# Every engine and the DMA queue held to one planned order over four batches' attention and channel MLPs

## The chip, the cores and the metric

The kernel runs on one core of one Trainium2 chip. The metric is the device time of one execution in microseconds (us), the median of three runs. A difference under 0.2% (1.75 us here) can't be told from none in this kernel.

## The reference, cut to what matters

Four batches, 768 positions, 8 heads of 48 columns (384 columns in all). First a linear attention with a complex decay: a state of 48x48 per head is turned and shrunk at each position by a normalised complex number, takes up `k v^T`, and is read by `q`:

```python
mag = np.sqrt(a_re * a_re + a_im * a_im)
scale = np.minimum(mag, 0.999) / (mag + 1e-06)
for t in range(S):
    new_re = ar * S_re - ai * S_im
    new_im = ar * S_im + ai * S_re
    S_re, S_im = (new_re + kv, new_im)
    y[:, :, t] = np.einsum('bhd,bhde->bhe', q[:, :, t], S_re)
```

Then two mixers on `x` (the attention's output, batch x 768 x 384). The first adds a product of rank 32 over positions and runs a channel MLP of four times the width; the second mixes positions by cosines and sines of `x @ w_theta` and ends with a narrow channel product:

```python
u = x + (x^T @ U @ V)^T
x = u + np.maximum(u @ w_ch1, 0.0) @ w_ch2
theta = x @ w_theta
y = w_tok_r @ (x * cos(theta)) + w_tok_i @ (x * sin(theta))
u = x + y
out = u + np.maximum(u @ w_ch, 0.0)
```

## The kernel before, in words

**Attention.** Positions are cut into 24 chunks of 128 (six per batch) and handled in 12 pairs of chunks, three per batch. For each pair `load` brings `a_re`, `a_im`, `q`, `k` in by DMA, and `ew` turns the recurrence into ordinary products by some twenty elementwise steps that pass between VectorE (L337 products, L340 fused ones, L358 and L385 running products and sums) and ScalarE (L334: squares, reciprocal roots, arc tangent and sines, which need two different function tables). All pairs but one work in the same buffer `er`; pair 1 has its own in `wa` and `wb`. At a pair's end, four rotations (L337) and the gathers (L405, L407, L409, DMAs on SP) put `q` and `k` into the tile `QK`, one per chunk. Then `pe_steps` runs the chunk on TensorE: scores (L453), transposed keys (L469), the state's update (L492), the values read (L521), a transpose back (L535), and `gx` (L546), which gathers `x @ U`. After six chunks `g_steps` adds the product of rank 32 to the batch: one small VectorE step (L568), then six products (L576) and six sums (L581).

**Channel MLP.** `mlp_steps(b)` cuts a batch into three blocks of 256 positions. A block's prologue (L682) transposes `x`; then come six F units, each 18 matmuls into a hidden tile (L711), whose result ScalarE (`rh`, L716) and VectorE (`rl`, L721) split into a high and a low part, and six C units of 12 matmuls (L736) that bring it back to 384 columns. The 9 pieces of `w_ch1` and 12 of `w_ch2` come as 64-bit words and are unpacked by VectorE and ScalarE in pieces (`unpack`, L609 to L622, L311).

**What sets the order.** `startup` makes a list of steps, each with the engines that may run it, a size and what it reads and writes. `schedule` places them one after the other by a model of the engines (`COST`, `HOP`): among the steps that can start within a short window it takes the one of the lowest rank, and a rank is the step's depth in the list plus a number from the table `LEAD`. `fixed` then issues the steps in that order, and ties each engine in `HELD` to it. Before, the list holds batches 0 and 1 of the attention, the unpacking of the weights, and the MLP of batch 0 (`PLANNED = 2`), and `HELD` is VectorE, ScalarE and GpSimd. TensorE and the DMA queue of SP are ordered by the recording layer's own scheduler, by priorities (`lane`). So is everything in batches 2 and 3 (`attention(b)`) and in the MLPs of batches 1 to 3 (`mains(b)`).

**The second mixer** (L908 to L993) starts when the MLPs are nearly through. Its weights are unpacked (lane `w3`) after the last attention step, beside the MLPs of the last batches.

Of the kernel before, what the change touches and what calls it, by code (L numbers as in the profile page):

```python
# [56 lines left out]
PLANNED = 2  # L57
# [30 lines left out]
def schedule(steps, rank, bias, hop=HOP, window=400):  # L88
# [20 lines left out]
    while ready:  # L109
        cand, low = [], 1e18  # L110
        for n in ready:
# [33 lines left out]
        at[e], end[n] = en, en + hop[e]  # L145
# [14 lines left out]

def ranks(steps, names, lead, hop=HOP):
# [27 lines left out]
def attn_moe_kernel(tc, pk, qn, kn, v, are, aim, U, V, w1, w2, wth, wtr, wti, wch, out):  # L189
# [26 lines left out]
    stg = [xf[:, PLANNED * NC * C + i * 1536:PLANNED * NC * C + (i + 1) * 1536] for i in range(3)]  # L216
# [44 lines left out]
    wa = wp.tile([128, KF * C], F32, tag="w", name="wa")  # L261
    wb = wp.tile([128, KF * C], F32, tag="w", name="wb")
    e_store = dict(key="E", lo=er[:, 0:5], hi=er[:, 5:])

    w_store = dict(key="W", **{n: t[:, 0:5 * NR].rearrange("p (z n) -> p z n", z=5) for n, t in (("lo", wa), ("hi", wb))})
    for st in (e_store, w_store):
# [10 lines left out]
        G_.memset(st["rows"][8][:, :, 0:1], 0.0)  # L277

# [9 lines left out]
    def load(pr, st):  # L288
# [4 lines left out]
        for z, name in enumerate(("re", ROWS[zi], "q", "kk")):  # L293
# [4 lines left out]
            ops.append(step(f, "D", 1300, [], [(st["key"], st["names"].get(name, name))]))  # L298
        return ops

    def load_v(g):
# [6 lines left out]
        return step(f, "D", 1300, [], [f"vt{g % 2}"])  # L308
# [6 lines left out]
    def ew(pr, st):  # L315
# [44 lines left out]
        do("A", 6, K("A"), [("pc", pr)], lambda e: A_.copy(out=pcf[:, pr], in_=rows[4][:, :, T]))  # L360
# [27 lines left out]
        act(AF.Identity, n2, Bt, bias=b_magic, r=K("B"), w=K("n"), size=N + 100)  # L388
# [21 lines left out]
        for i, g in enumerate((2 * pr, 2 * pr + 1)):  # L410
            ew_state[g] = {}
            for cs, to, a, keys in ((1, "cd", n2, ("C", "D")), (0, "qk", Bt, ("q", "kk"))):
# [4 lines left out]
                do("D", 3250, kc + K(*keys), [f"qk{g % 2}{cs}"], lambda e, g=g, cs=cs: gather(e, g, cs))  # L417
# [10 lines left out]
    def pe_steps(g, gps):  # L428
# [47 lines left out]
        for i in range(2):  # L476
            m = bank()
# [723 lines left out]
```

## Time and profile before

| | us |
|---|---|
| median of 3 runs | 877.26 (877.17 to 877.90) |
| the profiled execution | 877.16, of which 875.4 are the span |
| TensorE busy in the span | 757.8 (87%) |
| VectorE busy | 524.9 (60%) |
| ScalarE busy | 453.3 (52%) |
| GpSimd busy | 124.3 (14%) |

Engines are PE (TensorE matmul), PEld (its weight loads, beside PE), DVE (VectorE), ACT (ScalarE), POOL (GpSimd) and SP (the DMA queue). In a row of stretches stand the stretch and its length, then the busy time of each engine with its instructions in brackets, then the granted clock of TensorE as a share of full speed, the mean busy share of the 16 DMA engines, and GB/s. A row of instructions gives start, length, engine, line, operation, tiles, shapes and count, and in square brackets the idle time before it and what ended it. A row of waits gives who waited for whom, the sum, the times and the longest. A matmul of 32-bit numbers is counted twice in the trace, one of the rounded 32-bit kind (L711, L736) once.

### The profile page before, as it was taken

Reading aid. Unit: us, or ns where it says so; the run is one execution under the profiler, and the core shown is the slowest. Engines: PE = TensorE matmul, PEld = TensorE weight load, DVE = VectorE, ACT = ScalarE, POOL = GpSimd, SP = SyncE. Lnnn points to the kernel's source line nnn. Section 1 sums busy time; section 2 is a strip of 40 time slices with the busy share of each in tenths; the row PEclk is TensorE's granted clock in tenths of the full one; section 3 lists DMA queues with packets and bytes.
Section 4 is the critical chain, followed back from the end, with each engine's and each line's share of the span. In section 5 each row is a group of like instructions: output and inputs, shape, how many; then the busy total and the mean of one; then the engine's idle time right before and its main releaser. Section 6 shows DMA issues by size and latency. Waiting matters only on the chain.

```text
span 875.4 us, 13800 instructions
## 1 busy us (share of the span) xinstructions
PE 757.8 (87%) x5338; PEld 717.1 (82%) x5338; DVE 524.9 (60%) x787; ACT 453.3 (52%) x772; POOL 124.3 (14%) x144
## 2 busy tenths in 40 slices
PE   0085588798989698989999999899999999999996
PEld 0075367686978698979999999899999999999996
DVE  6958988978819578668151587893244335253321
ACT  6965876757726976784433253444155345253300
POOL 1011010200000002010101000000064234133200
PEclk9995867999998799999999999999999999999999
DMA  9264463552332443540331137620060000000001
GB/s 259 75 177 122 115 184 82 161 165 75 91 91 55 118 119 82 128 113 19 95 87 27 55 128 266 212 99 1 1 218 1 28 28 27 1 28 28 28 28 31
DMA packets 105657, 79.78 MB, mean 91 GB/s; under 512 B 32912, under 2 KB 97424, under 8 KB 105584
## 3 DMA queue, kind: packets, MB, share of 16 engines
q1 hardware_dynamic: 105184, 78.62, 32.2%
q8 instruction: 44, 0.72, 0.3%
q10 hardware_dynamic: 400, 0.20, 0.1%
q14 instruction: 29, 0.24, 0.1%
HBM read 50.33 MB, written 9.44 MB: 68 GB/s over the span
## 4 chain that ended last, share of the span: by engine, by line
PE 59%; DVE 15%; ACT 10%; DMA 8%; issue 3%; SPq 3%; POOL 0%; DVEq 0%; ACTq 0%; POOLq 0%
PE h L711 10%; PE c L736 9%; PE h L971 9%; PE c L971 9%; PE m L920 4%; PE m L987 4%; DVE er L337 4%; PE m L453 4%; PE m L521 4%; DMA er<-in_pk_dram 2%; ACT er L334 2%; DVE er L340 2%; PE m L492 2%; DMA tok1l<-tl 2%; ACT L334 2%
## 5 line engine op out<-in xcount | busy, mean ns | idle before, releaser
L711 PE MATMUL h<-uh,w1h 128*128 128x256 f32 x432 | 126.8, 294 | 3.1 <-DVE rl L721 2.1
L711 PE MATMUL h<-ul,w1h 128*128 128x256 f32 x432 | 125.0, 289 | 1.4 <-DVE ul L692 1.4
L711 PE MATMUL h<-uh,w1l 128*128 128x256 f32 x432 | 124.3, 288 | 0.0
L463 POOL TENSOR_SCALAR_AFFINE_SELECT pt<-pt 128x512 f32<-128x512 f32 x48 | 45.8, 962 | 425.7 <-ACT pt L459 411.2
L337 DVE TENSOR_TENSOR er<-er 128x768 f32<-128x768 f32 (+1 forms) x99 | 101.9, 1054 | 4.0 <-ACT er L334 2.0
L736 PE MATMUL c<-w2h,rl 128*128 128x384 f32 x288 | 100.1, 348 | 4.1 <-DVE rl L721 4.0
L736 PE MATMUL c<-w2h,rh 128*128 128x384 f32 x288 | 95.6, 349 | 6.7 <-ACT rh L716 3.0
L736 PE MATMUL c<-w2l,rh 128*128 128x384 f32 x288 | 97.8, 342 | 1.2 <-DVE w2l L311 1.1
L721 DVE SCALAR_TENSOR_TENSOR rl<-h,rh 128x512 fp32r<-128x512 f32 x72 | 49.3, 685 | 78.8 <-ACT rh L716 78.8
L711 PEld LDWEIGHTS h<-uh,w1h 128*128 128x128 f32 x432 | 83.5, 193 | 6.1 <-DVE rl L721 2.7
L711 PEld LDWEIGHTS h<-ul,w1h 128*128 128x128 f32 x432 | 83.6, 193 | 1.9 <-DVE ul L692 1.6
L711 PEld LDWEIGHTS h<-uh,w1l 128*128 128x128 f32 x432 | 83.5, 193 | 0.4 <-issue 0.2
L334 ACT ACTIVATE er<-er 128x768 f32<-128x768 f32 x88 | 74.0, 845 | 16.0 <-DVE er L337 12.4
L716 ACT ACTIVATE rh<-h 128x512 fp32r<-128x512 f32 x72 | 42.8, 596 | 67.4 <-PE h L711 59.5
L453 PE MATMUL m<-QK 96*128 96x128 f32 x384 | 60.0, 303 | 10.9 <-DMA QK<-wa 8.8
L453 PEld LDWEIGHTS m<-QK 96*128 96x128 f32 x384 | 53.5, 211 | 15.3 <-issue 10.5
L340 DVE SCALAR_TENSOR_TENSOR er<-er 128x768 f32<-128x768 f32 x55 | 52.8, 966 | 20.2 <-ACT er L334 11.6
L469 PE MATMUL m<-ident,QK 96*128 96x96 f32 x160 | 22.8, 261 | 46.0 <-DMA QK<-er 44.3
L736 PEld LDWEIGHTS c<-w2h,rh 128*128 128x128 f32 x288 | 52.8, 190 | 9.5 <-ACT rh L716 3.9
L736 PEld LDWEIGHTS c<-w2h,rl 128*128 128x128 f32 x288 | 54.6, 190 | 6.5 <-DVE rl L721 6.0
L469 PEld LDWEIGHTS m<-ident,QK 96*128 96x128 f32 x160 | 18.2, 150 | 49.6 <-issue 48.6
L736 PEld LDWEIGHTS c<-w2l,rh 128*128 128x128 f32 x288 | 54.3, 189 | 2.3 <-DVE w2l L311 1.8
(209 smaller groups left out, 1741.3 us busy)
## 6 DMA issues: line engine op xcount, KB each, us to landing
er<-in_pk_dram SPq DMA_DIRECT2D x88, 192.0 KB, 3.7
QK<-er SPq DMA_DIRECT2D x88, 145.1 KB, 3.4
x<-in_moe_w_ch_dram SPq DMA_DIRECT2D x9, 512.0 KB, 4.4
vt<-in_v_dram SPq DMA_DIRECT2D x48, 96.0 KB, 2.7
x<-in_moe_w_ch_dram SPq DMA_DIRECT2D x12, 384.0 KB, 3.4
st<-in_moe_w_tok_i_dram SPq DMA_DIRECT2D x6, 768.0 KB, 5.6
st<-in_moe_w_tok_r_dram SPq DMA_DIRECT2D x6, 768.0 KB, 4.2
out_dram<-x SPq DMA_DIRECT2D x23, 192.0 KB, 2.3
```

Source lines behind the costliest of these rows:

```text
L334: do("A", size, r, w, lambda e: A_.activation(out=out, in_=in_, func=func, **kw), tab)
L337: do("V", size, r, w, lambda e: V_.tensor_tensor(out=out, in0=in0, in1=in1, op=op))
L340: do("V", size, r, w, lambda e: V_.scalar_tensor_tensor(out=out, in0=in0, scalar=scalar, in1=in1, op0=op0, op1=op1))
L453: PE.matmul(ps[:, hh * T:(hh + 1) * T], lhsT=st["QK"][:, h, 1, 0:T], rhs=st["QK"][:, h, 0, 0:T], start=True, stop=True)
L463: G_.affine_select(out=pt, in_=pt, pattern=[[0, 4], [1, T]], compare_op=ALU.is_ge, fill=0.0, base=0, channel_multiplier=-1)
L469: PE.transpose(ps[:, hh * 96:(hh + 1) * 96], st["QK"][:, 4 * i + hh, 1, 0:T], ident[0:96, 0:96])
L521: PE.matmul(st["y"][64 * z:64 * z + 64, r * T:(r + 1) * T], lhsT=wide(old_w if k else vt_w, h), rhs=st["QK"][:, h, 0, 0:T] if k else st[f" ...
L711: PE.matmul(ps[:, f, :], lhsT=a[:, k, fs], rhs=u[:, k, :], start=(k == 0 and i == 0), stop=(k == NJ - 1 and i == 2))
L716: A_.activation(out=rh, in_=rts[n, p], func=AF.Relu)
L721: V_.scalar_tensor_tensor(out=rl, in0=ps, scalar=0.0, in1=r32(rh), op0=ALU.max, op1=ALU.subtract)
L736: PE.matmul(chs[n, t][:, 0:C], lhsT=r[:, f, t * T:(t + 1) * T], rhs=w[:, k, :], start=(k == 0 and i == 0), stop=(k == KF - 1 and i == 2))
L971: PE.matmul(ps[k][:, 0:C], lhsT=z[:, 2 * part + o, k * 128:(k + 1) * 128], rhs=w[:, s, ts], start=(s == 0 and part == 0 and j == 0), stop= ...
```

## The change

`PLANNED` becomes 4: the list holds the attention of all four batches and all four MLPs, and `attention` and the calls of `mains` fall away. `HELD` now has TensorE and SP too, so all five queues follow one order until the MLP of batch 3 is through. The table `LEAD` is new, with a number pair for every job of the longer list.

Smaller parts: DMA steps have a time to landing of their own in the model, and some costs in it are other (GpSimd's select, the transposes, the unpacking's first step); a scores tile is taken only while another tile of its pool stays free; new keys (`gord`, `fo`, `co`, the block's number in `u`) keep steps of one kind in turn; the copies of `x` in batches 2 and 3 name the staging space of the weights that lies under them (`stages`); `wa` and `wb` are declared at the size that they use. One step of each pair, the rounding of the angle (L388, 768 columns), may now run on VectorE: in the new order 7 of 12 do.

```diff
-    'l0': (17.6, 55.3), 'e0': (1.2, 0.1), 'p0': (-49.1, -22.6), 'u': (-11.1, 38.3), 'x0': (283.2, 62.0),
...
+    'l0': (692.3, 517.6), 'e0': (-3475.0, 1033.3), 'p0': (-2365.3, -705.0), 'u': (1406.8, -988.4),
...
-PLANNED = 2
+STAGED = 2
+
+PLANNED = 4
...
-                if not free:
+
+                if len(free) < 1 + (new[0][0] == "ps" and len(new[0]) > 2):
                     continue
...
-        at[e], end[n] = en, en + hop[e]
+        at[e], end[n] = en, en + (steps[n][5] if e == "D" and steps[n][5] else hop[e])
...
+    def stages(b, c):
+
+        i = ((b - STAGED) * NC + c) * C
+        return sorted({("s0", "h0", "h1")[j // 1536] for j in (i, i + C - 1)}) if b >= STAGED else []
...
-        act(AF.Identity, n2, Bt, bias=b_magic, r=K("B"), w=K("n"), size=N + 100)
+        do(EL, (N + 100) / 2, K("B"), K("n"), lambda e: V_.tensor_scalar(
+            out=n2, in0=Bt, scalar1=MAGIC, scalar2=None, op0=ALU.add) if e == "V" else
+            A_.activation(out=n2, in_=Bt, func=AF.Identity, bias=b_magic))
...
-    HELD = ('DVE', 'Activation', 'Pool')
+    HELD = ('DVE', 'Activation', 'Pool', 'PE', 'SP')
     def fixed(steps):
...
-    def attention(b):
-        gps = {}
-        for pr in range(b * NQ, (b + 1) * NQ):
-            run(load(pr, e_store))
-            run(ew(pr, e_store))
-            for g in (2 * pr, 2 * pr + 1):
-                a, m = pe_steps(g, gps)
-                run(a + m)
-        run(g_steps(b, gps))
-
...
-        for b in range(PLANNED):
+        for b in range(B):
...
-        ops = mlp_steps(0)
-        steps.extend(ops)
-        names.extend("m0" if o[1] == "P" else "mv" for o in ops)
+        for b in range(PLANNED):
+            ops = mlp_steps(b)
+            steps.extend(ops)
+            names.extend(MAIN[b] if o[1] == "P" else f"mv{b or ''}" for o in ops)
...
     for b in range(B):
-        if b + 1 < B:
-            for n in range(max(b + 1, PLANNED), b + 2):
-                with lane(f"a{n}"):
-                    attention(n)
-        else:
+        if b == B - 1:
...
-        if b:
+        if b >= PLANNED:
             mains(b)
```

What moves shows best at two places. The first is TensorE's queue where the MLP of batch 0 starts. Before, these rows stand at the end of its first F unit (L711) and show what comes next; L469 and L453 are the keys and scores of batch 1's first chunk:

```order
L711 MATMUL h<-ul,w1h 128x256
L711 MATMUL h<-uh,w1h 128x256
L711 MATMUL h<-uh,w1l 128x256
L711 MATMUL h<-ul,w1h 128x256
L469 MATMUL m<-ident,QK 128x96 x2
L453 MATMUL m<-QK 128x128 x2
L469 MATMUL m<-ident,QK 128x96 x4
L453 MATMUL m<-QK 128x128
L711 MATMUL h<-uh,w1h 128x256
L711 MATMUL h<-uh,w1l 128x256
```

Now two F units (L746 is the new number of L711) stand in one piece, and the first half of a C unit (L771, which was L736) comes next, then an F unit again:

```order
L746 MATMUL h<-uh,w1h 128x256
L746 MATMUL h<-uh,w1l 128x256
L746 MATMUL h<-ul,w1h 128x256
L771 MATMUL c<-w2h,rh 128x384
L771 MATMUL c<-w2h,rl 128x384
L771 MATMUL c<-w2l,rh 128x384
L771 MATMUL c<-w2h,rh 128x384
L771 MATMUL c<-w2h,rl 128x384
L771 MATMUL c<-w2l,rh 128x384
L746 MATMUL h<-uh,w1h 128x256
```

The keys and scores of batch 1's first chunk moved back behind 8 F units and 5 C units of batch 0's MLP, and every unit or half unit now stands unbroken.

The second place is VectorE's queue around L568, the step that ends batch 0's attention. Before, the step stands behind elementwise work of the next pair (`er`) and a piece of `w_ch1` (x and `w1l` at 512 columns):

```order
L391 TENSOR_SCALAR carry<-er 128x3
L337 TENSOR_TENSOR er<-er 128x6x128
L610 TENSOR_SCALAR x<-x 128x512
L611 TENSOR_SCALAR x<-x 128x512
L613 SCALAR_TENSOR_TENSOR x<-x 128x512
L337 TENSOR_TENSOR er<-er 128x3x2x128
L615 SCALAR_TENSOR_TENSOR x<-x 128x512
L568 TENSOR_TENSOR g_859<-gps,g_859 32x384
L311 TENSOR_TENSOR w1l<-x,w1h 128x512
L581 TENSOR_TENSOR x<-x,m 128x384 x6
```

Now (L603 is the new number of L568) pieces of `w_ch2` (384 columns) stand there:

```order
L650 SCALAR_TENSOR_TENSOR x<-x 128x512
L645 TENSOR_SCALAR x<-x 128x384
L646 TENSOR_SCALAR x<-x 128x384
L344 TENSOR_TENSOR w1l<-x,w1h 128x512
L648 SCALAR_TENSOR_TENSOR x<-x 128x384
L650 SCALAR_TENSOR_TENSOR x<-x 128x384
L603 TENSOR_TENSOR g_867<-gps,g_867 32x384
L344 TENSOR_TENSOR w2l<-x,w2h 128x384
L616 TENSOR_TENSOR x<-x,m 128x384 x6
L727 TENSOR_TENSOR ul<-up,uh 128x512
```

Ahead of this step stood one finished piece of `w_ch2` and now stand four; the elementwise work of batch 1 moved the other way, behind it.

## Rows read from the trace of the kernel before

**Rows 1.** The page's chain of work that ended last, by engine.

```profile
PE 59%; DVE 15%; ACT 10%; DMA 8%; issue 3%; SPq 3%; POOL 0%; DVEq 0%; ACTq 0%; POOLq 0%
```

**Rows 2.** Stretches by stage; PE, PEld, DVE, ACT, POOL busy; clock; DMA.

```profile
0.00:142.00 142.00, 66.25 (x445) 53.77 (x445) 114.41 (x162) 103.74 (x159) 15.27 (x36) 0.82 0.58 148
142.00:260.00 118.00, 105.26 (x832) 95.28 (x832) 84.73 (x132) 71.32 (x124) 10.48 (x12) 0.96 0.44 118
260.00:292.00 32.00, 29.31 (x179) 28.16 (x180) 30.69 (x41) 22.97 (x36) 0.16 (x1) 0.84 0.26 68
292.00:495.00 203.00, 189.29 (x1586) 176.87 (x1585) 113.63 (x154) 113.20 (x192) 23.28 (x24) 0.97 0.32 80
495.00:642.00 147.00, 141.97 (x982) 138.53 (x981) 92.20 (x144) 56.30 (x91) 4.01 (x5) 1.00 0.38 126
```

**Rows 3.** TensorE in order of time: batch 0's start, batch 3's last sum product.

```profile
135.98 2.52 PE L576 MATMUL m<-g,v 96*128 96x384 f32 x6 [1.46 <-DVE g L568]
...
141.96 0.58 PE L711 MATMUL h<-uh,w1h 128*128 128x256 f32 x1
...
494.85 0.34 PE L576 MATMUL m<-g,v 96*128 96x384 f32 x1
```

**Rows 4.** Stretch 142 to 495, F units' matmuls (L711) alone: PE busy.

```profile
142.00:495.00 353.00, 110.75 (x763) 0.96 0.35 92
```

**Rows 5.** The same stretch, C units' matmuls (L736) alone.

```profile
142.00:495.00 353.00, 102.68 (x492) 0.96 0.35 92
```

**Rows 6.** Chain of waits in order of time: a C and an F unit, unbroken.

```profile
591.85 2.11 PE c L736 x12
...
602.88 2.14 PE h L711 x18
```

**Rows 7.** Stretches, VectorE alone: length, busy (count), clock, DMA.

```profile
135.37:246.50 111.13, 90.40 (x142) 0.93 0.44 119
135.37:259.57 124.20, 90.40 (x142) 0.94 0.43 116
259.57:487.51 227.94, 140.64 (x187) 0.96 0.32 81
...
150.00:200.00 50.00, 42.36 (x69) 0.93 0.57 158
```

**Rows 8.** Waits of VectorE between 142 and 292.

```profile
DVE g L568 <- ACT g L565: 13.1, 1, 13.1
```

**Rows 9.** Waits of VectorE between 292 and 495.

```profile
DVE rl L721 <- ACT rh L716: 44.5, 12, 6.3
...
DVE er L340 <- DMA QK<-er: 3.6, 1, 3.6
```

**Rows 10.** Chain of waits in order of time: a pair's last gather.

```profile
287.34 0.62 SPq L405
...
288.00 0.60 SPq L407
...
288.65 1.92 DMA QK<-er
```

**Rows 11.** ScalarE in order of time, a change of function table.

```profile
291.73 1.28 ACT L334 ACT_TABLE_LOAD   x1
293.02 0.85 ACT L334 ACTIVATE er<-er 128x768 f32<-128x768 f32 x1
```

**Rows 12.** TensorE in order of time: a wait, and a change of work.

```profile
299.16 0.47 PE L492 MATMUL m<-vt,kn 128*96 128x96 f32 x1 [6.86 <-ACT kn L422]
...
305.01 0.37 PE L711 MATMUL h<-uh,w1h 128*128 128x256 f32 x1
305.21 0.28 PE L711 MATMUL h<-uh,w1l 128*128 128x256 f32 x1
```

**Rows 13.** Groups by line and form: count, busy us, mean ns, idle before.

```profile
L337 DVE TENSOR_TENSOR er<-er 128x768 f32<-128x768 f32 x88 | 82.8, 966 | 2.8 <-ACT er L334 2.0 <-ACT er L371 0.2
...
L334 ACT ACTIVATE er<-er,cb 128x768 f32<-128x768 f32 x33 | 30.6, 931 | 12.1 <-DVE er L385 11.9
...
L380 DVE TENSOR_SCALAR er<-er 128x768 f32<-128x768 f32 x2 | 1.1, 550 | 0.0
```

More of the change, by code (lines that the diff above doesn't have):

```diff
@@ L127, in schedule @@
                 if e == "P":
-                    d = (1.05 if tab else 1.25) * size
+                    d = (1.05 if tab else 1.1) * size
                     if st - at[e] > 3400:
@@ L158, in schedule, with batch_of @@
     return sorted(out)
+MAIN = [f"m{b}" for b in range(PLANNED)]
+def batch_of(name):
+    per = {"l": NQ, "e": NQ, "p": NC, "x": NC, "g": 1}.get(name[0])
+    return int(name[1:]) // per if per and name[1:].isdigit() else 0
 def ranks(steps, names, lead, hop=HOP):
@@ L215, in attn_moe_kernel @@
     xf = xall.rearrange("p b c d -> p (b c d)")
-    stg = [xf[:, PLANNED * NC * C + i * 1536:PLANNED * NC * C + (i + 1) * 1536] for i in range(3)]
+    stg = [xf[:, STAGED * NC * C + i * 1536:STAGED * NC * C + (i + 1) * 1536] for i in range(3)]
     ident = const.tile([128, 128], F32, name="ident")
@@ L260, in attn_moe_kernel @@
     er = ac.tile([128, len(ROWS), NR], F32, name="er")
-    wa = wp.tile([128, KF * C], F32, tag="w", name="wa")
-    wb = wp.tile([128, KF * C], F32, tag="w", name="wb")
+    wa = wp.tile([128, 5, NR], F32, tag="w", name="wa")
+    wb = wp.tile([128, 5, NR], F32, tag="w", name="wb")
     e_store = dict(key="E", lo=er[:, 0:5], hi=er[:, 5:])
-    w_store = dict(key="W", **{n: t[:, 0:5 * NR].rearrange("p (z n) -> p z n", z=5) for n, t in (("lo", wa), ("hi", wb))})
+    w_store = dict(key="W", lo=wa, hi=wb)
     for st in (e_store, w_store):
@@ L297, in f @@
                     nc.sync.dma_start(out=to, in_=pk[b, 2 * c + i, :, z])
-            ops.append(step(f, "D", 1300, [], [(st["key"], st["names"].get(name, name))]))
+            ops.append(step(f, "D", 1300, [], [(st["key"], st["names"].get(name, name))], 2400))
         return ops
@@ L307, in f @@
                 nc.sync.dma_start(out=vt[:, :, 2 * z, :], in_=v[b, z::2, c * T:(c + 1) * T, :].rearrange("r s e -> s r e"))
-        return step(f, "D", 1300, [], [f"vt{g % 2}"])
+        return step(f, "D", 1000, [], [f"vt{g % 2}"], 2400)
     def tt(e, **kw):
@@ L359, in ew @@
             out=flat(4), data0=flat(8), data1=d1.rearrange("p j c t -> p (j c t)"), initial=0.0, op0=ALU.mult, op1=ALU.add))
-        do("A", 6, K("A"), [("pc", pr)], lambda e: A_.copy(out=pcf[:, pr], in_=rows[4][:, :, T]))
+        do("A", 6, K("A"), [("pcf", pr)], lambda e: A_.copy(out=pcf[:, pr], in_=rows[4][:, :, T]))
         act(AF.Abs_reciprocal_sqrt, Dt, P2, "R", r=K("A"), w=K("D"))
@@ L416, in ew @@
                     K("q", "kk", ("q", i), ("kk", i), "nB"[cs == 0]), K(*(keys if i == 0 else ())) + kc)
-                do("D", 3250, kc + K(*keys), [f"qk{g % 2}{cs}"], lambda e, g=g, cs=cs: gather(e, g, cs))
+                do("D", 3250, kc + K(*keys), [f"qk{g % 2}{cs}"], lambda e, g=g, cs=cs: gather(e, g, cs), 1450)
         return ops
@@ L526, in pe_steps @@
         for i in range(2):
-            do("P", 1000 if c else 500, qk + [vk, f"pt{i}"] + ([ko] if c else []), [m], lambda e, i=i: yt(e, i))
+            do("P", 870 if c else 440, qk + [vk, f"pt{i}"] + ([ko] if c else []), [m], lambda e, i=i: yt(e, i))
         def ycp(e):
@@ L551, in pe_steps @@
             mring[0] += 1
-            gps["k"] = ("ps", mring[0])
+            gps["k"] = ("ps", mring[0], 1)
         gk = [gps["k"]] if b else []
         mix.append(step(lambda e: copy(e, xs[b][:, c, :].rearrange("p (h d) -> p h d", d=D),
-                                       st["y"].rearrange("p (h d) -> p h d", d=64)[:, :, 0:D]), "A", 384, [m], [m, ("x", b, c)]))
-        mix.append(step(gx, "P", 660, [("x", b, c), "u4"], [kg] + gk))
+                                       st["y"].rearrange("p (h d) -> p h d", d=64)[:, :, 0:D]), "A", 384, [m], [m, ("x", b, c)] + stages(b, c)))
+        mix.append(step(gx, "P", 660, [("x", b, c), "u4"], [kg] + gk + ["gord"] * (c == 0)))
         return ops, mix
@@ L571, in g_steps @@
         ops.append(step(g4, "A", 384, [("gps", b) if b else "gps"] + gk, ["pt1"]))
-        ops.append(step(g4l, "V", 384, [("gps", b) if b else "gps", "pt1"], ["pt1"] + gk))
+        ops.append(step(g4l, "V", 384, [("gps", b) if b else "gps", "pt1"], ["pt1", "gord"] + gk))
         def hx(e, i):
@@ L607, in unpack @@
         do("D", 650 * reps + n * 2, load)
-        do(EU, n / 2, lambda e: V_.tensor_scalar(out=t, in0=w_hi, scalar1=0x7FFFFFFF, scalar2=None, op0=ALU.bitwise_and) if e == "V" else
+        do(EU, n + 70, lambda e: V_.tensor_scalar(out=t, in0=w_hi, scalar1=0x7FFFFFFF, scalar2=None, op0=ALU.bitwise_and) if e == "V" else
            A_.activation(out=tf, in_=w_hi.bitcast(F32), func=AF.Abs), wt)
@@ L721, in lo @@
                 V_.scalar_tensor_tensor(out=rl, in0=ps, scalar=0.0, in1=r32(rh), op0=ALU.max, op1=ALU.subtract)
-            do("P", 18 * 119, [("u", n % 2)] + [("w1", p // 2, k) for k in range(NJ)], [m], mm)
+            do("P", 18 * 119, [("u", (b * NB + n) % 2)] + [("w1", p // 2, k) for k in range(NJ)], [m, "fo"], mm)
             do("A", 512, [m], [kr], hi)
```

15 lines of the change are left out of this document (8 added, 7 removed), and 38 rows, old and new, of the table LEAD.

## The prediction, made before the changed kernel ran

> **What bounds the kernel now.** I read the chain of waits first, then the busy time by stage, then TensorE's own order of time, and last VectorE. TensorE holds 59% of the chain, VectorE 15% [rows 1], so the question of each stage is what keeps TensorE from matmuls. The stages [rows 2] differ. Up to 142 us TensorE is busy for 66 us only, since it waits for the first batch's elementwise work. From 142 us, where the first F matmul starts [rows 3], it has MLP work to fill with: it idles 12.7 us of the next 118, 2.7 of 32, 13.7 of 203, and 5.0 of the 147 up to 642. Behind 642 the second mixer keeps it full, and the change leaves that part as it is.
>
> Idle time is not the whole loss. The granted clock in the three stretches between 142 and 495 is 0.96, 0.84 and 0.97 [rows 2], so some of the time ran at the lower of its two levels; against full speed that is 0.04 x 118 + 0.16 x 32 + 0.03 x 203 = 4.7 + 5.1 + 6.1 = 15.9 us. With the idle time, 29.1 us, TensorE loses 45.0 of the 353 us, and 308.0 us is what the work itself takes. That is the room of the change: batch 3's last sum product ends at 495 [rows 3], and from there the last 380.5 us have little left to win.
>
> Why does TensorE wait there? VectorE's largest wait between 142 and 292 is one of 13.1 us at L568 [rows 8]. Its queue was held to a plan, TensorE's was not, and TensorE came to the last `gx` of batch 1 later than the plan of VectorE had it. VectorE stood with the pairs of batch 2 behind that step. Later TensorE in turn waits 6.86 us for these pairs, through ScalarE [rows 12].
>
> **The change, part by part.**
>
> *The same work, counted.* I counted both orders from the first F matmul to batch 3's last sum product. Before there are 763 F and 492 C matmuls in it, as the trace has them too [rows 4, 5]; now 756 and 486. An unbroken F unit takes 2.14 us for 18, 0.119 each, a C unit 2.11 for 12, 0.176 each [rows 6], so 0.8 + 1.1 = 1.9 us of work goes behind that point. The runs of one kind of work in the stretch fall from 320 to 260. A change of work costs about 0.20 - 0.12 = 0.08 us, from the first two F matmuls after a transpose [rows 12], so 60 of them give 4.8 us. The work is then 308.0 - 1.9 - 4.8 = 301.3 us, and what follows 380.5 + 1.9 = 382.4.
>
> *The start.* Ahead of batch 0's L568 VectorE has 150 instructions before and 160 now. With each form's mean duration of this trace they sum to 115.5 and 115.2 us. The weights' pieces and the pairs have only changed places, so I leave the first F matmul at 142. An error here moves the end one for one; I allow 8 us either way.
>
> *Holding TensorE, with 8 F and 5 C units moved ahead of batch 1's first scores.* This fills TensorE from 142 on and makes the attention of batch 1 later. So VectorE decides: can it bring the pairs in time? The tightest place in the new order is batch 1's third pair. Ahead of it TensorE has 15 F units, 14 C units and four chunks of attention. A chunk, with its share of the small products, is what is left of the work: (308.0 - 763 x 0.119 - 492 x 0.176) / 18 = 7.3 us. That makes 15 x 2.14 + 14 x 2.11 + 4 x 7.3 = 90.7 us, and TensorE would be there at 232.7 without any wait. VectorE has 136 instructions from L568 to that pair's last rotation, 103.4 us by the same durations. The same count for the 142 instructions before batch 1's L568 gives 97.0 where the trace has 90.4 busy [rows 7], as neighbours overlap a little, so I take 103.4 x 90.4/97.0 = 96.4 us of busy time.
>
> What share of the time will VectorE be busy? The rows give 0.81 (90.40 of 111.13, up to the long wait), 0.73 with the wait in it, 0.85 in its densest 50 us, 0.62 behind it [rows 7], and 0.96 in the 32 us in which it had a backlog [rows 2]. In the new order it has a backlog through this stretch, but still hands work to ScalarE and back, so I take 0.85; 0.62 and 0.96 are the ends. Then the pair ends at 135.4 + 96.4/0.85 = 248.8, where 135.4 is the start of L568 [rows 7]. Its last gather takes 0.62 + 0.60 + 1.92, with the pauses 3.2 us [rows 10], and TensorE goes on at 252.0, 19.3 us of waits behind it.
>
> *From there on* the counts ask less of VectorE: to the ends of the next four pairs TensorE's own work always comes out as the later of the two at 0.85. TensorE has 301.3 - 90.7 = 210.6 us left to batch 3's last sum product, which comes to 462.6. Handovers stay: in the last 203 us of the stretch before, 13.7 us idle, of which I take the one of 6.86 to go and 6.8 to stay, and of the 6.1 us of clock loss the same share, 3.0. So 462.6 + 9.8 = 472.4.
>
> *Holding SP.* The DMAs are as many as before. VectorE waits for one only once in the later stretch, for 3.6 us [rows 9], so I cost the new order of the queue at nothing. What hides a late load is the pair before it in work. With that cover gone a gather that waits in the queue holds the next pair's load behind it; then 3.6 us is the price for each pair, 29 us for the 8 pairs behind 142 as the upper end, and 0 to 4 is what I take.
>
> *The rounding step on VectorE.* 7 of 12 move: 7 x 0.55 us on VectorE, 7 x 0.93 less on ScalarE [rows 13]. VectorE's part is in the counts above. The other edits (the smaller tiles, the staging names, the rule on free tiles, the model's costs) change only what the plan allows, and have no instruction of their own.
>
> *ScalarE's tables.* Between the L568 of batch 0 and that of batch 3 the order has 27 loads of a function table where it had 23. A load takes 1.28 us and the next step starts 0.01 us behind its end [rows 11]: 4 x 1.28 = 5.1 us on an engine that is idle for 145 of 353 us [rows 2], so I add nothing for them. The Trainium skill (ScalarE: Activation LUTs, "What ACT_TABLE_LOAD costs") speaks harder against such an order: it puts a drain of about 1.38 us behind each load, 2.66 us in all, which would make 10.6 us of the four. The trace does not show that drain, and by the page too ScalarE's idle time would hide the loads.
>
> *The sum*, against the profiled execution: 472.4 + 382.4 = 854.8 us of span, and the 1.8 us around it (877.16 less 875.4) make 856.6, say 857. The profiled execution is 0.1 us under the median, so this stands for the median too.
>
> **The rivals.**
>
> *TensorE alone is the bound.* If VectorE runs at 0.96 the pair ends at 135.4 + 100.4 = 235.8, TensorE waits 6.3 us there, and with 3 us of handovers batch 3's products end at 142 + 301.3 + 9.3 = 452.6: 835 + 1.8 = 837 us. With no loss at all it would be 827.5. For it speaks the stretch 260 to 292, against it that 0.96 held for 32 us only.
>
> *Nothing is gained.* At 0.73, VectorE's share with the long wait in it, the pair ends at 267.5, TensorE goes on at 270.7 and the sum is 270.7 + 210.6 + 9.8 + 382.4 + 1.8 = 875. This is the case if one plan for all queues meets the same kind of wait, VectorE at the head of its queue for a product that TensorE has not reached. For it: the plan is a model's, and the long wait before was at a planned step. Against it: the other side of that wait was unplanned then.
>
> *Slower.* VectorE is held at `rl`. This step of the MLP waits for ScalarE's half, which waits for an F unit, and cost 44.5 us in 12 waits in the later stretch [rows 9]. The elementwise work of the next pair stands behind it in the queue, and TensorE's queue, now held too, can't take something else when that pair is late: the two wait for each other in turn. VectorE's share there was 0.62; with it the third pair ends at 290.9 and the sum is 294.1 + 604.6 = 899. The point from which it decides is a share of 0.72. Against it: in that stretch TensorE was nearly full, and VectorE had little to hurry for.
>
> *The change does not do what it says* is hardly open: the new order shows TensorE and SP in the plan's sequence.
>
> **How the numbers follow.** A difference under 0.2%, 1.75 us, counts as none. I give the likeliest case 0.48 (846 to 868, shares of VectorE from 0.78 to 0.90), TensorE alone 0.18 (827 to 846), the case without gain 0.14 (868 to 880) and the slower one 0.20 (880 to 900). Faster gets the first two and half of the third, 0.73; within 0.2% 0.05; slower 0.22, with the rest of the third. The range leaves out about 0.05 below 832 and 0.13 above 888.
>
> **What would show it.** In the changed kernel's profile the first F matmul stands at 134 to 150; VectorE's busy share between the L568 steps of batches 0 and 1 (L603 there) is 0.8 or more, with no wait of 10 us at that step; TensorE's longest waits fall before the scores of batch 1's third pair, some 20 us in sum, and behind it idle time is under 10 us; batch 3's last sum product ends near 472, and 384 us follow. The forecast is wrong if VectorE's share is under 0.72, if the time from that last product to the end is not within some 4 us of before, or if the start has moved by more than 8 us.

## The result and the profile after

The changed kernel takes 844.79 us (median of 4 runs, 842.76 to 847.19), the kernel before 877.58 us in the same comparison. The ratio is 0.9625, with an interval of 0.9595 to 0.9655: the change saves 32.8 us, where 20 were forecast. The profiled execution of the changed kernel took 847.19 us, the longest of the four, with a span of 845.5; the rows below are of this execution.

The chain of waits of the changed kernel, by engine, against [rows 1]:

```profile
PE 53%; DVE 15%; DMA 11%; SPq 7%; ACT 7%; issue 5%; POOL 1%; DVEq 0%; ACTq 0%; POOLq 0%
```

Its stretches by stage, cut at the points that answer to those of [rows 2, 3]: the first F matmul, the scores of batch 1's third pair, batch 3's last sum product. The columns are length, busy time (count) of PE, PEld, DVE, ACT and POOL, granted clock, DMA share and GB/s.

```profile
0.00:136.00 136.00, 60.21 (x447) 50.90 (x447) 116.17 (x174) 96.36 (x152) 13.66 (x36) 0.86 0.62 163
136.00:236.00 100.00, 95.54 (x743) 90.40 (x742) 91.50 (x125) 77.29 (x124) 7.05 (x8) 0.96 0.38 102
236.00:463.40 227.40, 219.11 (x1840) 201.44 (x1841) 146.90 (x198) 132.81 (x222) 25.20 (x28) 1.00 0.37 93
463.40:845.50 382.10, 370.44 (x2314) 366.75 (x2312) 180.53 (x303) 141.67 (x265) 75.00 (x72) 0.99 0.21 69
```

The gain lies where it was looked for. Between the first F matmul and batch 3's last sum product TensorE idles 12.7 us (4.5 and 8.3), where it was 29.1 [rows 2], and in 227 of these 327 us the granted clock is 1.00. The last stretch has hardly moved, 382.1 us against 380.5. The chain has turned a little from TensorE to the transfers (DMA and SPq together 18%, 11% before). Why is not shown; TensorE's own waits for a gather sum to only 1.0 us from 136 to 465.

TensorE in order of time, against [rows 3] (start, duration, operation, output and input, what it waited for):

```profile
129.06 2.48 PE L611 MATMUL m<-g,v 96*128 96x384 f32 x6 [2.38 <-DVE g L603]
...
135.91 0.58 PE L746 MATMUL h<-uh,w1h 128*128 128x256 f32 x1
...
463.37 0.34 PE L611 MATMUL m<-g,v 96*128 96x384 f32 x1
```

The start came 6.1 us earlier, the last sum product 31.5 us. The waits of VectorE from 128 to 260, the attention of batches 0 and 1, against [rows 8] (engine, what it waited for, us in total, times, longest):

```profile
DVE er L373 <- ACT er L367: 4.3, 2, 3.4
DVE rl L756 <- ACT rh L751: 4.0, 4, 2.8
...
DVE g L603 <- ACT g L600: 1.7, 1, 1.7
```

And from 260 to 465, against [rows 9]:

```profile
DVE a_st L538 <- PE m L527: 24.9, 6, 9.0
DVE rl L756 <- ACT rh L751: 10.8, 7, 3.3
...
DVE g L603 <- ACT g L600: 4.6, 1, 4.6
```

The 13.1 us at L568 (L603 now) are 1.7, the 44.5 us at `rl` 10.8. VectorE still waits for TensorE, 24.9 us in six waits at `a_st`, the step that adds TensorE's product to the state. That costs little, because TensorE is full meanwhile: its own largest waits from 136 to 465 are these, and none is over 2 us, where [rows 12] had one of 6.86.

```profile
PE m L570 <- ACT yT L566: 3.4, 3, 1.7
PE h L746 <- DVE rl L756: 2.0, 1, 2.0
PE m L556 <- POOL pt L498: 1.9, 3, 1.2
PE m L527 <- ACT kn L457: 1.3, 1, 1.3
```

### The profile page after: what moved, and what is told of

Its sections match the earlier page's. It is cut to its first block, busy times and chain, and to the rows that moved or that the text cites. A ratio compares the mean times of both kernels' runs of the same rounds, so it can differ in the third digit from the quotient of the medians.

```text
span 845.5 us, 13778 instructions
## 1 busy us (share of the span) xinstructions
PE 745.3 (88%) x5338; PEld 709.5 (84%) x5338; DVE 535.1 (63%) x797; ACT 448.1 (53%) x762; POOL 120.9 (14%) x144
## 4 chain that ended last, share of the span: by engine, by line
PE 53%; DVE 15%; DMA 11%; SPq 7%; ACT 7%; issue 5%; POOL 1%; DVEq 0%; ACTq 0%; POOLq 0%
PE h L993 9%; PE c L993 9%; PE h L746 8%; PE c L771 7%; PE m L942 4%; PE m L1009 4%; DVE er L370 4%; PE m L488 3%; PE m L556 3%; SPq L440 3%; DMA er<-in_pk_dram 2%; ACT er L367 2%; SPq L444 2%; DMA tok1l<-tl 2%; DMA QK<-er 2%
## 5 line engine op out<-in xcount | busy, mean ns | idle before, releaser
L746 PE MATMUL h<-uh,w1h 128*128 128x256 f32 x432 | 126.3, 292 | 5.4 <-DVE rl L756 5.3
L746 PE MATMUL h<-ul,w1h 128*128 128x256 f32 x432 | 124.1, 287 | 0.0
L746 PE MATMUL h<-uh,w1l 128*128 128x256 f32 x432 | 123.9, 287 | 0.0
L370 DVE TENSOR_TENSOR er<-er 128x768 f32<-128x768 f32 (+1 forms) x99 | 104.3, 1072 | 10.8 <-ACT er L367 3.8
L771 PE MATMUL c<-w2h,rh 128*128 128x384 f32 x288 | 103.5, 359 | 0.3 <-DVE x L776 0.3
L498 POOL TENSOR_SCALAR_AFFINE_SELECT pt<-pt 128x512 f32<-128x512 f32 x48 | 42.6, 895 | 405.6 <-ACT pt L494 399.8
L771 PE MATMUL c<-w2h,rl 128*128 128x384 f32 x288 | 97.7, 339 | 0.4 <-DVE rl L756 0.3
L771 PE MATMUL c<-w2l,rh 128*128 128x384 f32 x288 | 97.3, 338 | 0.0
L746 PEld LDWEIGHTS h<-uh,w1h 128*128 128x128 f32 x432 | 83.6, 193 | 8.1 <-DVE rl L756 6.8
L746 PEld LDWEIGHTS h<-ul,w1h 128*128 128x128 f32 x432 | 83.7, 194 | 0.2 <-DVE ul L727 0.2
L746 PEld LDWEIGHTS h<-uh,w1l 128*128 128x128 f32 x432 | 83.7, 194 | 0.1
L488 PE MATMUL m<-QK 96*128 96x128 f32 x384 | 56.3, 298 | 13.3 <-DMA QK<-wa 11.1
L488 PEld LDWEIGHTS m<-QK 96*128 96x128 f32 x384 | 51.3, 208 | 17.0 <-issue 13.4
L373 DVE SCALAR_TENSOR_TENSOR er<-er 128x768 f32<-128x768 f32 x55 | 53.1, 967 | 15.4 <-ACT er L367 10.7
L504 PE MATMUL m<-ident,QK 96*128 96x96 f32 x160 | 20.5, 261 | 47.7 <-DMA QK<-er 46.8
L504 PEld LDWEIGHTS m<-ident,QK 96*128 96x128 f32 x160 | 16.9, 148 | 49.5 <-issue 47.4
L771 PEld LDWEIGHTS c<-w2h,rh 128*128 128x128 f32 x288 | 54.3, 189 | 3.4 <-issue 2.3
L771 PEld LDWEIGHTS c<-w2h,rl 128*128 128x128 f32 x288 | 54.4, 189 | 2.0 <-DVE rl L756 0.9
L771 PEld LDWEIGHTS c<-w2l,rh 128*128 128x128 f32 x288 | 54.2, 188 | 0.0
```

The lines of the kernel that those rows point to most:

```text
L370: do("V", size, r, w, lambda e: V_.tensor_tensor(out=out, in0=in0, in1=in1, op=op))
L373: do("V", size, r, w, lambda e: V_.scalar_tensor_tensor(out=out, in0=in0, scalar=scalar, in1=in1, op0=op0, op1=op1))
L488: PE.matmul(ps[:, hh * T:(hh + 1) * T], lhsT=st["QK"][:, h, 1, 0:T], rhs=st["QK"][:, h, 0, 0:T], start=True, stop=True)
L498: G_.affine_select(out=pt, in_=pt, pattern=[[0, 4], [1, T]], compare_op=ALU.is_ge, fill=0.0, base=0, channel_multiplier=-1)
L504: PE.transpose(ps[:, hh * 96:(hh + 1) * 96], st["QK"][:, 4 * i + hh, 1, 0:T], ident[0:96, 0:96])
L746: PE.matmul(ps[:, f, :], lhsT=a[:, k, fs], rhs=u[:, k, :], start=(k == 0 and i == 0), stop=(k == NJ - 1 and i == 2))
```

## The experiments

The theory (A): the gain is that TensorE follows the same sequence as VectorE, so neither stands at the head of its queue for a step that the other has put off. The rivals: the gain is the order table itself, the later MLPs in the plan, the SP queue, or only the relief of VectorE. Each kernel was compared with the kernel before on its own chip (medians there 874.5 to 875.8), so across chips the ratios are what compares. The runs of the changed kernel alone lie up to 6 us apart (841.43 to 847.26), so a difference of 2 or 3 us between two medians is not read here, though it is more than 0.2%.

### TensorE and SP free in the new list

```diff
-    HELD = ('DVE', 'Activation', 'Pool', 'PE', 'SP')
+    HELD = ('DVE', 'Activation', 'Pool')
```

> The changed kernel with TensorE and SP not held to the plan, as before the change; VectorE, ScalarE and GpSimd keep the new order. Theory A (holding TensorE to the same plan as VectorE is what removes the waits): most of the gain goes, the time is 858 to 872 us, and VectorE shows waits of 5 us or more at the steps that end a batch's attention (L603) or at the state's update (L538). Theory B (the new table and the longer list set VectorE's order, and that order alone brings the gain): 842 to 849 us, as the changed kernel.

869.95 us (867.41 to 871.88), ratio 0.9945 (0.992 to 0.9971). By the ratios 28 of the 32.8 us are gone with this one line. VectorE's longest waits between 120 and 480 in that kernel, and the first of them in the next kernel, where TensorE is held:

```profile
DVE a_st L538 <- PE m L527: 46.0, 10, 13.1
DVE rl L756 <- ACT rh L751: 15.7, 10, 4.5
```

```profile
DVE a_st L538 <- PE m L527: 27.0, 8, 9.2
```

A wait of 13.1 us for TensorE is back, now at `a_st`: TensorE reaches a product later than VectorE's plan has it, as before at L568. Up to 136 us ScalarE shows the same at `yT`, again first with TensorE free and then with TensorE held:

```profile
ACT yT L566 <- PE m L556: 10.6, 3, 7.0
```

```profile
ACT yT L566 <- PE m L556: 5.5, 3, 2.3
```

One thing is left open: the table came with a plan that holds TensorE. What a table made for a free TensorE would reach on this list was not tried.

### SP alone free

```diff
-    HELD = ('DVE', 'Activation', 'Pool', 'PE', 'SP')
+    HELD = ('DVE', 'Activation', 'Pool', 'PE')
```

> The changed kernel with SP alone not held; all compute engines keep the plan's order. I costed the held queue at nothing: then the time is within 2 us of the changed kernel's 845. If holding the queue had a part in the gain (loads that come in time), it is slower by 4 us or more; if it had a price (a gather that holds the next pair's load), faster by 3 us or more.

843.63 us (843.05 to 844.04), ratio 0.9649 (0.9633 to 0.9665): not told apart from the changed kernel. Between this kernel and the one above, run on one chip, only TensorE's hold differs, so 26.3 us (869.95 less 843.63) are TensorE's alone. On the new list holding SP costs and brings nothing that shows.

### TensorE and SP held in the kernel before

```diff
-    HELD = ('DVE', 'Activation', 'Pool')
+    HELD = ('DVE', 'Activation', 'Pool', 'PE', 'SP')
```

> The kernel before (its short list and old table) with TensorE and SP held too, inside that list. Theory A: the wait of 13.1 us at the end of batch 1's attention goes or falls under 4, and the time falls by 8 to 16 us, to 861 to 869. Theory B: within 4 us of 877, since the list and the table are the old ones.

865.01 us (862.21 to 866.38), ratio 0.9883 (0.9858 to 0.9908): about 10 us faster, the size that theory A had, but not mainly where it had them. One part of the expectation missed: the wait at L568 should have fallen under 4 us. The waits of VectorE up to 292 and, in the second fence, behind it:

```profile
DVE g L568 <- ACT g L565: 9.3, 1, 9.3
```

```profile
DVE rl L721 <- ACT rh L716: 46.7, 12, 7.2
```

The wait shrank to 9.3 us only, though batch 1's L568 came 17 us sooner (242.7, not 259.6), and the 44.5 us at `rl` [rows 9] stayed. And by the account further down, 7.6 of the profile's 10.7 us lie ahead of the first F matmul, where VectorE's longest wait is not for TensorE but for the gathers of pair 1. It reads, before and then with both queues held:

```profile
67.72 0.96 DVE L337 TENSOR_TENSOR wb<-wa,wb 128x768 f32<-128x768 f32 x1 [9.46 <-DMA QK<-wb]
```

```profile
63.09 0.96 DVE L337 TENSOR_TENSOR wb<-wa,wb 128x768 f32<-128x768 f32 x1 [4.10 <-DMA QK<-wb]
```

So on the old list a part of the 10 us may be SP's; no run holds TensorE alone there. What the rest of the gain needs is an order made for it.

### The old table on the new list

The numbers of the table that sets the order are taken from the kernel before, all else is the changed kernel. For batches 2 and 3 and the later MLPs the old table has no numbers; they get a default.

```diff
-    'l0': (692.3, 517.6), 'e0': (-3475.0, 1033.3), 'p0': (-2365.3, -705.0), 'u': (1406.8, -988.4),
+    'l0': (17.6, 55.3), 'e0': (1.2, 0.1), 'p0': (-49.1, -22.6), 'u': (-11.1, 38.3), 'x0': (283.2, 62.0),
...
```

> The changed kernel, all engines and SP held and the list over four batches, with the old table of numbers (batch 2 and 3 and the later MLPs get the default). Theory L (holding and the longer list bring the gain, the table only tunes it): 843 to 853 us. Theory T (the new table brings what holding the old list did not): 858 us or more.

907.32 us (906.05 to 909.46), ratio 1.0359 (1.0326 to 1.0393), 63 us above the changed kernel. VectorE waits for 103 us at `rl` (L742 here, the lines stand 14 lower) between 130 and 570, in 32 waits, and batch 3's attention ends 101 us later. That looks like the prediction's slower rival. But the long waits and the loss lie apart. The waits at `rl` from 137 to 400 and, in the second fence, from 400 to 565:

```profile
DVE rl L742 <- ACT rh L737: 13.7, 5, 5.8
```

```profile
DVE rl L742 <- ACT rh L737: 86.2, 26, 8.6
```

The same two stretches, columns as above:

```profile
137.40:400.00 262.60, 213.63 (x1646) 191.75 (x1645) 202.16 (x275) 180.18 (x284) 24.73 (x28) 0.90 0.43 110
400.00:564.70 164.70, 164.12 (x1243) 160.40 (x1243) 49.54 (x79) 39.46 (x74) 5.08 (x8) 0.99 0.09 21
```

Where VectorE stands at `rl`, TensorE is full with MLP work (164.1 of 164.7 us). TensorE idles 49 us ahead of that, at a clock of 0.90, spread over many waits: the largest sums up to 400 are 7.8 us for `rl`, 6.8 for a gather, 6.4 for `ul` and 5.4 for a piece of `w_ch2`. So a held order can be much worse than none, and the new table is what avoids it; that the waits at `rl` are what it loses by is not what this run shows.

### The MLPs of batches 2 and 3 outside the list

```diff
-PLANNED = 4
+PLANNED = 2
```

> The changed kernel with the MLPs of batches 2 and 3 out of the list (their order is the recording layer's, as before); all else held, new table. In the new order those MLPs come almost wholly behind the last attention product, where TensorE is full anyway: 842 to 849 us if only the order up to there matters. If the plan of the late MLPs has a part in the gain: 852 or more.

852.46 us (850.77 to 854.86), ratio 0.9744 (0.9709 to 0.9779): 8 us slower than the changed kernel by the medians, 10 by the ratios. The expectation left 849 to 852 undecided; the measured time falls just into the case in which the later MLPs have a part in the gain, and with runs from 850.77 to 854.86 that is no clear verdict. Its waits of VectorE from 134 to 500, and the stretch to batch 3's last sum product:

```profile
DVE rl L756 <- ACT rh L751: 42.7, 18, 6.3
```

```profile
134.10:499.60 365.50, 348.75 (x2812) 327.49 (x2811) 249.20 (x340) 209.74 (x349) 29.78 (x36) 0.98 0.34 86
```

Here the table is used on a list that it was not made for, so the 8 to 10 us hold both, the later MLPs and the misfit; the run doesn't part them.

### VectorE loaded early, late, and relieved

Four more products of 128x768 in each of three pairs, whose results are not used: pairs 3 to 5 (batch 1) in one kernel, 9 to 11 (batch 3) in the other.

```diff
-        stt(m2, sq, M2_MAX, m2, ALU.min, ALU.mult, K("dec", "sq"), K("dec"))
+        def m2_step(e):
+            V_.scalar_tensor_tensor(out=m2, in0=sq, scalar=M2_MAX, in1=m2, op0=ALU.min, op1=ALU.mult)
+            for _ in range(4 if pr in (3, 4, 5) else 0):
+                V_.tensor_tensor(out=sq, in0=sq, in1=sq, op=ALU.mult)
+        do("V", N, K("dec", "sq"), K("dec"), m2_step)
```

> The changed kernel with 4 extra VectorE products in each pair of batch 1 (12 of 768 columns, some 10.5 to 11.5 us in all, on a row that is no longer read), the order else as it was. If VectorE sets the time up to batch 1's third pair, as the prediction had it, that pair's scores come 8 to 11 us later and the end 6 to 10 us later (851 to 855). If TensorE is the bound there, the end moves by 3 us at most.

> The changed kernel with the same 4 extra VectorE products per pair as in the early case, but in the pairs of batch 3. Theory V (VectorE binds up to batch 1's third pair, TensorE behind it): the end moves by 4 us at most, to 844 to 849. Rival (VectorE sets the time in every batch, since it waits in turn with TensorE): 10 us or more, as in the early case, where 11 us of extra work cost 16 to 18.

Early: 861.82 us (856.65 to 864.96), ratio 0.9838 (0.9792 to 0.9884), 16 to 19 us for 12.4 us of work (groups of 3.94, 4.56 and 3.94 us). Late: 850.88 us (847.51 to 855.22), ratio 0.9724 (0.9675 to 0.9772), 5 to 9 us. The early price is higher than expected (6 to 10 us), the late one between the two expectations. So VectorE bounds early and has more room late, as the counts said, but not as cleanly. The early loss is 3.8 us at the start, 7.7 us of TensorE's idle time and 6.1 us of clock, by the account further down. How a step off TensorE's path becomes idle time shows in the trace: first VectorE's row of one group (175.97 is its start), then ScalarE's rows behind it, then TensorE's.

```profile
175.97 4.56 DVE L393 TENSOR_TENSOR er<-er 128x768 f32<-128x768 f32 x4
```

```profile
180.57 0.84 ACT L367 ACTIVATE er<-er 128x768 f32<-128x768 f32 x1 [4.30 <-DVE er L393]
...
184.85 0.56 ACT L570 COPY yT<-m 128x512 f32<-128x512 f32 x1
```

```profile
185.46 1.12 PE L574 MATMUL m<-ident,yT 128*128 128x128 f32 x4 [5.33 <-ACT yT L570]
```

ScalarE stood 4.30 us at the head of its held queue for the pair, and the copy `yT`, which TensorE's next products need and which has nothing to do with the pair, came behind it; TensorE waited 5.33 us for it. In a plan held on every engine one late step delays its queue, and then the queues that read from it. One of the groups (at 123.6) also fell ahead of batch 0's last VectorE step (at 132.3), so the start came later too.

The other way, two steps of the refinement are left out in pairs 3 to 5, 5.8 us less on VectorE:

```diff
-        stt(Ct, Ct, -0.5, P2, ALU.mult, ALU.mult, K("C", "A"), K("C"))
-        stt(Dt, Ct, 1.5, Dt, ALU.add, ALU.mult, K("C", "D"), K("D"))
+        lean = pr in (3, 4, 5)
+        do("V", N, K("C", "A"), K("C"), lambda e: None if lean else V_.scalar_tensor_tensor(
+            out=Ct, in0=Ct, scalar=-0.5, in1=P2, op0=ALU.mult, op1=ALU.mult))
+        do("V", N, K("C", "D"), K("D"), lambda e: None if lean else V_.scalar_tensor_tensor(
+            out=Dt, in0=Ct, scalar=1.5, in1=Dt, op0=ALU.add, op1=ALU.mult))
```

> The changed kernel without two VectorE products in each pair of batch 1 (the step that refines the reciprocal root is left out there; 6 products, 5.8 us). If TensorE is now full in this stretch (4.5 us idle between 136 and 236 in the changed kernel), the end comes 0 to 4 us earlier. If the stretch is set by VectorE in both directions, 5 to 8 us earlier.

842.87 us (839.79 to 847.47), ratio 0.9638 (0.9589 to 0.9686), not told apart from the changed kernel. So VectorE stands just at the edge here: more work on it costs at once, less brings nothing that shows, since TensorE has only the 12.7 us of idle time left to give.

### The start: subtractions moved to GpSimd

Ahead of the first F matmul VectorE is busy for 116 of 136 us. Nine subtractions of the unpacking of `w_ch1` go to GpSimd; in a second kernel the twelve of `w_ch2` too. The changed kernel ran again beside them.

```diff
-        do("V", n, lambda e: tt(e, out=lo, in0=tv, in1=r32(hi), op=ALU.subtract), w)
+        low = "G" if wt and wt[0][0] in ("w1",) else "V"
+        do("V", n, lambda e: tt(low, out=lo, in0=tv, in1=r32(hi), op=ALU.subtract), w)
```

> The changed kernel once more, on the chip of the next three, as their measure: 842 to 847 us by every theory.

> The changed kernel with the 9 subtractions that make the low part of w_ch1 on GpSimd in place of VectorE (0.76 us each, 6.9 us, all ahead of batch 0's L603 or just behind it), in the same places of the plan. Theory V (VectorE's queue up to L603 sets when TensorE can start its MLPs, and the time behind is TensorE's own work plus small waits): the first F matmul comes 4 to 7 us earlier and the end 3 to 7 us earlier than the changed kernel. Rival (the start is set by the chain of a pair through VectorE and ScalarE, and these steps fill gaps): within 2 us.

> The same with the 12 subtractions of w_ch2 on GpSimd too (0.555 us each, 6.7 us, most behind batch 0's L603). Theory V: 1 to 3 us faster than with w_ch1 alone, since behind L603 TensorE idles only some 4.5 us up to batch 1's third pair. Rival (GpSimd's slower subtractions hold the selects of the scores behind them): 2 us or more slower than with w_ch1 alone.

The same kernel again: 845.6 us (841.43 to 847.26), ratio 0.9649 (0.9627 to 0.9671). With `w_ch1`: 847.14 us (844.8 to 853.04), ratio 0.9683 (0.9654 to 0.9711). With both: 849.07 us (847.31 to 852.41), ratio 0.9701 (0.968 to 0.9723). The 3 to 7 us that were to be gained are not there, and the second kernel is not told apart from the first. The rival's number came (within 2 us), but not as a test of it, since VectorE was not relieved: it has nine instructions fewer up to 136 us, but is busy for longer, 118.2 us where the changed kernel's first stretch above has 116.2:

```profile
0.00:136.00 136.00, 59.82 (x447) 49.36 (x447) 118.23 (x165) 96.10 (x152) 31.08 (x45) 0.86 0.62 163
```

The time went into VectorE's other steps. In the first of the two kernels, GpSimd's rows and then VectorE's at the same time; the third fence is the same VectorE step in the changed kernel (durations in ns):

```profile
44.83 1.26 POOL L344 TENSOR_TENSOR w1l<-x,w1h 128x512 fp32r<-128x512 f32 x1 [10.20 <-ACT w1h L657]
...
56.57 2.54 POOL L344 TENSOR_TENSOR w1l<-x,w1h 128x512 fp32r<-128x512 f32 x1 [1.49 <-ACT w1h L657]
```

```profile
56.01 2.03 DVE L418 TENSOR_TENSOR_SCAN wb<-ones,carry,wa 128x257 f32<-128x257 f32 x3
57.96 1.96 DVE L373 SCALAR_TENSOR_TENSOR wb<-wb,wa 128x768 f32<-128x768 f32 x1
```

```profile
L373 DVE SCALAR_TENSOR_TENSOR wb<-wb,wa x1: 930/930/930, 57.8 to 57.8; 128x768 f32<-128x768 f32 x1
```

A subtraction on GpSimd takes 1.26 us at best. Beside VectorE's steps it took 2.54 us, and ended at 59.11; VectorE's step that began at 57.96 took 1.96 us instead of 0.93 and ended 0.81 us behind 59.11. By these times the two engines took turns. The Trainium skill (SBUF — State Buffer, "Who interferes with whom") says that a VectorE instruction with two inputs in SBUF and a GpSimd one that reads SBUF exclude each other for a whole instruction, whichever came first; the trace agrees, 1.96 against 0.93 us.

### The rounding back on ScalarE

```diff
-        do(EL, (N + 100) / 2, K("B"), K("n"), lambda e: V_.tensor_scalar(
+        do('A', N + 100, K("B"), K("n"), lambda e: V_.tensor_scalar(
```

> The changed kernel with the rounding step on ScalarE alone, as before; the plan is made anew from the same table and comes out in another order. If the step's engine matters by its own cost (3.9 us on VectorE against 6.5 on ScalarE): within 4 us of the changed kernel. If the table fits one list of steps only, so that a small change of the list spoils the order: 855 us or more.

861.06 us (858.24 to 862.92), ratio 0.982 (0.9799 to 0.9842), 16 us slower for seven instructions of 0.55 us, which ScalarE does in 0.93. The plan is made anew from the same table, and comes out worse: six other steps that may run on either engine moved from ScalarE to VectorE, and in its stretch to batch 3's last sum product TensorE idles 19.8 us and the clock is 0.97.

```profile
136.60:482.00 345.40, 325.65 (x2614) 299.81 (x2614) 235.07 (x320) 211.62 (x345) 30.53 (x36) 0.97 0.35 90
```

So the table, good on one list of steps, is not good on this neighbour of it. What the rounding itself is worth under a table of its own stays open.

### The kernels by one account

For profiled executions, in us. Loss is the span less the start (first F matmul) and less TensorE's own work from there on. That work is the rest of the span without the idle time and without half of the busy time at the lower level of the clock; so loss is idle time plus what the clock cost.

| kernel | start | batch 3's last sum product | TensorE idle between | work | loss | span |
|---|---|---|---|---|---|---|
| before | 142.0 | 494.8 | 29.1 | 681.2 | 52.2 | 875.4 |
| changed | 135.9 | 463.4 | 12.7 | 679.6 | 30.0 | 845.5 |
| changed, again | 133.2 | 461.3 | 14.6 | 681.7 | 29.4 | 844.3 |
| new list, SP free | 133.9 | 461.3 | 12.5 | 681.1 | 26.9 | 841.9 |
| new list, TensorE and SP free | 140.9 | 491.2 | 23.7 | 683.1 | 44.2 | 868.2 |
| before, all held | 134.4 | 479.8 | 25.6 | 679.9 | 50.4 | 864.7 |
| new list, old table | 137.4 | 564.7 | 49.5 | 678.7 | 91.7 | 907.8 |
| MLPs 2, 3 outside | 134.1 | 499.6 | 16.8 | 678.1 | 37.5 | 849.7 |
| VectorE loaded early | 139.7 | 481.6 | 19.7 | 679.7 | 43.8 | 863.2 |
| rounding on ScalarE | 136.6 | 481.5 | 19.8 | 681.0 | 43.5 | 861.1 |

The work is the same within 5 us in all of them, whatever the order; 22.2 of the 29.9 us of gain are loss, 6.1 are start, 1.6 work. The 1.6 are not told from none: the changed kernel's own two profiles differ by 2.1 in work. The start has a scatter of its own too, 135.9 in one profile and 133.2 in the other. TensorE's hold on the new list (SP free against both free) is 17.3 us of loss, 7.0 of start and 2.0 of work.

## Why the prediction came out as it did

**The mechanism was right.** The gain is TensorE's, it needs TensorE held to VectorE's sequence (26 us return when it is freed), and SP's hold was rightly costed at nothing on the new list. The hold alone does not bring it: with the old table the same hold loses. The counts of work held exactly, the F and C matmuls of the stretch (the lines are L746 and L771 now, in two fences as two views):

```profile
136.20:463.40 327.20, 100.87 (x756) 96.41 (x755) 0.99 0.37 95
```

```profile
136.20:463.40 327.20, 100.62 (x486) 83.65 (x487) 0.99 0.37 95
```

The tail came to 382.1 us, 382.4 forecast.

**VectorE's share was taken too low.** Its rows against [rows 7] (length, busy time and count of VectorE, clock, DMA):

```profile
128.44:234.92 106.48, 96.82 (x137) 0.93 0.37 102
128.44:259.08 130.64, 111.21 (x155) 0.94 0.40 107
259.08:459.68 200.60, 131.06 (x176) 1.00 0.36 90
```

The busy time up to batch 1's third pair is 96.8 us, 96.4 forecast; the share is 0.91, not 0.85. I had taken 0.85 because the new order still hands work to ScalarE and back. It does, but in a sequence that the two share, and no wait up to 260 is longer than 3.4 us. TensorE came to that pair's scores at 235.8 instead of 252.0. Of these 16.2 us 6.9 are the higher share and 7.0 the earlier start of VectorE's stretch (128.4, not 135.4). The other 2.3 are the gather: TensorE began with the pair's first chunk 0.9 us behind the end of the rotations at 234.9, not 3.2. The 19.3 us of waits that were to stand ahead of it were 4.5: this sign, which I had named to show the forecast right, failed. The last sum product, which was to end near 472, came at 463.4. On this point the rival "TensorE alone is the bound" (share 0.96, 6.3 us of waits) describes the kernel better than the likeliest case.

**The start** was left at 142 with 8 us allowed either way; it came 6.1 us earlier. With TensorE free it stands at 140.9 in the new list and 142.0 in the old, with it held at 135.9 and 134.4, and at 137.4 with the old table on the new list, so this is the hold's doing and not the table's. The prediction had put nothing for it: it summed VectorE's instructions ahead of L568, a sum that stayed the same, and not the waits between them.

**The work was mis-sized, and this hid the rest.** Start and waits alone would have put the kernel at 838. Idle time and clock together cost about 16.5 us in the stretch (12.7, and 3.8 of clock) where 29.1 were forecast (19.3 and 9.8). The work was 310.9 us, not 301.3. Two terms were wrong. First, the 308.0 us of before: I subtracted idle time and then the clock's share over all of the time, idle time included. Two stretches of the kernel before show it (columns as in [rows 2]; the clock was low from 294.2 to 304.4):

```profile
291.00:299.00 8.00, 1.30 (x12) 1.03 (x10) 0.98 (x3) 7.91 (x10) 1.27 (x2) 0.71 0.71 197
299.20:305.00 5.80, 5.39 (x36) 4.65 (x37) 4.25 (x6) 5.77 (x10) 0.00 (x0) 0.54 0.01 4
```

The clock fell while TensorE idled, and its low spell is partly idle time: in the first stretch TensorE works for 1.30 of 8.00 us, so a low clock costs it next to nothing there; in the second, busy for 5.39 of 5.80 us at 0.54, it costs nearly half. Of the 29.5 us at the lower level 8.7 were idle, so 4.3 us were counted twice. With another 1 us from the rounded clock shares, the work of before was about 313. Second, the 4.8 us for 60 fewer changes of work: counted by the lines of TensorE's matmuls behind the start, there are 509 runs of one kind of work in the kernel before and 443 in the changed one, and the work differs by 1.6 us. That would be 0.02 us for a change, not 0.08, and it is not told from none, as said above. The price was read from one pair of rows [rows 12], and the distance of two matmuls after a change is not what the change costs the whole stream.

So two errors met: 18.7 us too much in start and losses (6.1 and 12.6), 9.6 us too little in work, and 857 stands 10 us above the profiled 847. That it is not further off is luck. The range held the time, and the sign was right; the median, 844.79, lies just inside the case of TensorE alone (827 to 846).

**The rivals.** "Nothing is gained" asked for a wait at the head of VectorE's queue for TensorE. Such waits exist (24.9 us in six), but late, where VectorE has room. "Slower" did not happen here. With the old table a slower order came out at 907, but that this is close to the 899 it was given is, by that trace, chance: TensorE lost its time where the waits at `rl` were small, and was full where they were large. What the prediction did not see is how far the result hangs on the table: the list with the new table is 33 us faster than before, the same list with the old table 32 us slower.

## What to carry to other kernels

When one engine's queue is held to a plan, hold the engines that it waits for to the same plan, or the held one may stand waiting at the head of its queue (26 us here). But with all queues held a late step is passed on, so the plan has to be made for that list of steps and looked at again after each edit: one kind of step forced to another engine cost 16 us, an old table 63. To size such a change, write the time as start plus TensorE's fixed work plus idle time plus clock loss, and count the clock only over the time that TensorE is busy. Look at where the engine that waits has room, and whether the bounding engine idles there too: 25 us of VectorE's waits left TensorE full here, and 86 us of them did so under the old table.

## What was not expected of the hardware

- TensorE's work from the first F matmul to the end, net of idle time and clock, was 678 to 683 us in orders with 433 to 540 runs of one kind of work. No price of a change of kind shows above the scatter of one order (679.3 to 681.7 us in eight profiles with 443 runs).
- GpSimd and VectorE took turns: 9 subtractions moved off VectorE (9 x 0.68 = 6.2 us) left it 2 us busier, since its steps beside them took up to 1.96 us instead of 0.93.
- The same shows without any subtraction moved. Of the three groups of four products of 128x768 in the kernel loaded early, the one of 4.56 us ran while GpSimd had two selects (row below, from 175.39); beside no work of GpSimd a group took 3.94. In the kernel loaded late it was again the one group beside two selects that took 4.56.

```profile
175.39 2.35 POOL L502 TENSOR_SCALAR_AFFINE_SELECT pt<-pt 128x512 f32<-128x512 f32 x2 [54.47 <-ACT pt L498]
```

```profile
202.77 3.94 DVE L393 TENSOR_TENSOR er<-er 128x768 f32<-128x768 f32 x4
```
